# An attention and feed-forward kernel: P divided by products with a diagonal, weight bits decoded by way of PSUM, and two scalars loaded second

## The chip, the cores and the metric

The kernel runs on one core of a Trainium2 chip. The metric is the device time of one execution in microseconds (us). Each program was timed several times; one more execution was recorded by the hardware profiler, and every row shown below is from that record.

## What is computed

The reference in short (sizes of this case: B=4, H=8, S=768, D=64; 3072 tokens, d_model 512, d_ff 2048; n_local 96, n_global 8):

```python
scores = q @ k.T / sqrt(D)
keep = (pos_k < n_global) | ((rel >= 0) & (rel < n_local))      # rel = pos_q - pos_k
scores += -slope[h] * where(is_global & ~is_local, n_local, abs(rel))
a = softmax(where(keep, scores, -1e9))
x = (a @ v) as tokens x (H*D)                                    # 3072 x 512
h = x @ w_in
P = a0 + a1*h + a2*h**2 + a3*h**3
Q = 1 + |b0|*|h| + |b1|*h**2
out = (P / (Q + 1e-6)) @ w_out
```

The two weight matrices arrive as 64-bit floats; the kernel turns their bits into 32-bit floats itself. That is what "decode" means below.

## The kernel before

The work is cut into 96 attention units (u) and 96 feed-forward steps (f). A unit is one block of 128 queries of a pair of heads, in one batch. The blocks i = 0 to 5 of a batch follow each other, and only the block itself and the one before it hold keys to keep, beside the first eight keys. A chunk c is 256 tokens (two blocks, eight units); its feed-forward part is eight steps, each for 256 of the 2048 inner columns. A planner orders the instructions of every engine from priorities: the loop `windowed` runs over t, gives each stage of step t a priority 1000 t plus an offset (`PRI_A` while f is below 8, `PRI` after), and the planner takes what is ready, the lowest number first. The engines then run their lists in order. Step t holds the load of unit t+4, the score and softmax of unit t-2, the transposes of P of unit t-3, the product with V of the pair that ends at t-5, and feed-forward step f = t-12. So attention runs twelve steps ahead, and chunk 0's feed-forward steps fall into t = 12 to 19.

A unit goes like this. `st_load` brings q, k and v by DMA from the SP queue. `st_split` writes each number of q and k as two fp32r numbers (VectorE, then GpSimd at L370). `st_qkT` transposes them on TensorE, `st_qkE` copies them out on ScalarE. `st_score` makes the products (L408), and VectorE adds the mask and takes the row's minimum (L419). `st_soft` is the exponential on ScalarE (L429) and the reciprocal of the row's sum on VectorE (L432, L434). `st_norm` multiplies P by that reciprocal on GpSimd (L441), `st_pT` transposes P on TensorE (L462) and copies it out (L465, ScalarE while u is below 21), `st_pv` multiplies with V (L480). From unit 30 on (RAW) P is copied by a DMA, and its transposes are fp32r.

A feed-forward step: ffn1 (L250 for chunk 0 in fp32, L258 after that in three fp32r products) writes h into a PSUM tile of tag h, of which there are two; `st_ew1` to `st_ew4` make P/Q on ScalarE, VectorE and GpSimd, reading h until L290; ffn2 (L329, later L334) multiplies with w_out.

The weights come as 32 pieces of 128x512. `WSCHED` says in which step t a piece is loaded and decoded: numbers 0 to 5 in t = 0 and 2, 6 to 11 in t = 10, 12 to 17 in t = 11, and 18 to 31 in t = 12 to 18. `MODE` gives for each piece how it is decoded:

- mode 0 and 1: one step on ScalarE (L171), a guard on VectorE (mode 0) or GpSimd (mode 1) (L173), and three steps on VectorE (L174, L176, L178);
- mode 2 and 3: one step on ScalarE (L185), one on GpSimd (mode 2, L187) or ScalarE (mode 3, L189) that writes `low` over the loaded data, and two steps on VectorE (L190, L192).

A loaded piece stands in one of three buffers until its decode has read it. `split_w` later writes each piece as two fp32r pieces (L209, L210) for the chunks from 1 on; these run in step f, by the list `SPLITS`.

`windowed` begins with the loads of units 0 and 2, then n_local and n_global, the identity, the coefficients, two splits and the masks, before the loop. After the loop stands a check of n_local and n_global in small steps on one partition (L679 to L684), which decides whether a general path is run; the planner puts them where VectorE is free.

Of the kernel before, what the change touches and what calls it, by code (L numbers as in the profile page):

```python
# [18 lines left out]
G = 8  # L19
# [4 lines left out]
GBUFS = 3  # L24
RAW = 30
# [11 lines left out]
MODE = (3, 0, 2, 0, 2, 1, 2, 0, 0, 0, 0, 0, 0, 2, 2, 1, 0, 0, 0, 0, 0, 0, 0, 0, 2, 2, 1, 0, 3, 2, 1, 2)  # L37
# [33 lines left out]
def window_masks(nc, scr, mask0, masks, nl, ng):  # L71

    rel, msk, key, g1 = scr
    for n, base in ((0, P), (1, 0)):
# [5 lines left out]
        if n:  # L80
            nc.gpsimd.affine_select(out=rel, in_=rel, pattern=[[-1, P]], base=0, channel_multiplier=1,
                                    compare_op=ALU.is_ge, fill=-BIG)
        nc.vector.tensor_tensor(out=m, in0=rel, in1=msk, op=ALU.add)

    nc.gpsimd.iota(key[:, 0:G], pattern=[[1, G]], base=0, channel_multiplier=0,
                   allow_small_or_imprecise_dtypes=True)
    nc.vector.tensor_scalar(out=g1[:, 0:G], in0=key[:, 0:G], scalar1=ng, scalar2=nl, op0=ALU.is_lt, op1=ALU.mult)
    nc.vector.tensor_scalar(out=g1[:, G:2 * G], in0=key[:, 0:G], scalar1=ng, scalar2=-BIG, op0=ALU.is_ge, op1=ALU.mult)
    nc.vector.tensor_tensor(out=masks[:, 0, 0:G], in0=g1[:, G:2 * G], in1=g1[:, 0:G], op=ALU.subtract)
    nc.vector.tensor_copy(out=mask0, in_=masks[:, 1, :])  # L90
    nc.vector.tensor_tensor(out=mask0[:, 0:G], in0=mask0[:, 0:G], in1=masks[:, 0, 0:G], op=ALU.max)
# [4 lines left out]
def tile_kernel(ctx: ExitStack, tc: tile.TileContext, q, k, v, n_global, n_local,  # L96
# [30 lines left out]
    def st_load(u):  # L127
# [6 lines left out]
        vt = pl.ldp.tile([P, 4, D], F32, tag="vt", name=f"vt{u}", bufs=6)  # L134
        nc.sync.dma_start(out=vt, in_=v[b, hs, r, :].rearrange("h s d -> s h d"))
        nat[u // 2] = n
        vts[u // 2] = vt
# [20 lines left out]
    def decode(src, key):  # L158
# [26 lines left out]
        nc.scalar.activation(out=dst, in_=raw[:, :, 1], func=AF.Abs, scale=2.0 ** -112)  # L185
        if mode == 2:
            nc.gpsimd.tensor_scalar(out=low, in0=half, scalar1=2.0 ** -13, scalar2=FLOOR, op0=ALU.mult, op1=ALU.add)  # L187
        else:
            nc.scalar.activation(out=low, in_=half, func=AF.Copy, scale=2.0 ** -13, bias=FLOOR)  # L189
# [246 lines left out]
    def st_norm(u):  # L436
        i = unit(u)[4]
        pr, st = prob[u]
        for x in range(2):
# [15 lines left out]
    def st_pT(u):  # L455
# [4 lines left out]
        for x in range(2):  # L460
            for w in range(W):
                nc.tensor.transpose(out=t_ps[:, x, w, :], in_=pr[:, x, w, :], identity=ident_r if u >= RAW else ident)  # L462
# [43 lines left out]
    def windowed():  # L506
        st_load(0)
        st_load(2)
        nc.sync.dma_start(out=ni[:, 0:2], in_=n_local.bitcast(I32).partition_broadcast(P))
        nc.sync.dma_start(out=ni[:, 2:4], in_=n_global.bitcast(I32).partition_broadcast(P))  # L510
        make_identity(nc, ident)
        nc.vector.tensor_copy(out=ident_r, in_=ident)
        nc.vector.tensor_copy(out=nf, in_=ni)
        load_coef()
        st_split(0)
        st_split(1)

        nl, ng = nf[:, 0:1], nf[:, 2:3]
        scr = tmp("scr").rearrange("p a (b w) -> p (a b) w", w=P)
        scr = [scr[:, x, :] for x in range(4)]  # L520
        window_masks(nc, scr, mask0, masks, nl, ng)

        base = tc.cur_priority
        for t in range(NU + LAG + F2):
# [8 lines left out]
            if t % 2 == 0:  # L533
                on("load", st_load, t + 4)
            on("score", st_score, t - 2)
# [140 lines left out]
    fl = const.tile([1, 8], F32, name="fl")  # L676
    fi = const.tile([1, 1], I32, name="fi")
    for n, (x, lo, hi) in enumerate(((0, 1.0, 121.0), (1, 0.0, 0.0), (2, 0.0, float(G)), (3, 0.0, 0.0))):
        nc.vector.tensor_scalar(out=fl[:, 4:5], in0=nf[0:1, x:x + 1], scalar1=lo, scalar2=None, op0=ALU.is_ge)  # L679
        nc.vector.tensor_scalar(out=fl[:, 5:6], in0=nf[0:1, x:x + 1], scalar1=hi, scalar2=None, op0=ALU.is_le)  # L680
        nc.vector.tensor_tensor(out=fl[:, n:n + 1], in0=fl[:, 4:5], in1=fl[:, 5:6], op=ALU.mult)
    nc.vector.tensor_tensor(out=fl[:, 4:6], in0=fl[:, 0:2], in1=fl[:, 2:4], op=ALU.mult)
    nc.vector.tensor_tensor(out=fl[:, 6:7], in0=fl[:, 4:5], in1=fl[:, 5:6], op=ALU.mult)
    nc.vector.tensor_copy(out=fi, in_=fl[:, 6:7])  # L684
# [40 lines left out]
```

## Time and profile before

| | |
|---|---|
| time, median of 3 runs | 794.26 us (793.93 to 798.46) |
| time of the profiled execution | 792.2 us |
| its span | 790.4 us |
| TensorE busy | 743.9 us (94%) |
| TensorE weight loads busy | 649.6 us (82%) |
| VectorE busy | 599.6 us (76%) |
| ScalarE busy | 575.1 us (73%) |
| GpSimd busy | 533.3 us (67%) |

The span is the time between the first and the last instruction; the profiled execution's own time holds 1.8 us more. In the rows PE is TensorE, PEld its weight loads, DVE VectorE, ACT ScalarE, POOL GpSimd, SPq the queue that issues the DMAs. A number such as L441 is a line of the kernel. Names of tiles stand without their numbers, so `w_0f` to `w_15f` are decoded pieces, `r` a loaded one, `pr` P, `tp` its transposes. Busy time overlaps: matmuls are pipelined, so what one costs is better read from the distance between starts.

### The profile page before, as it was taken

What the parts mean: (1) busy time and instruction counts of PE and PEld (TensorE: products, weight loads), DVE (VectorE), ACT (ScalarE), POOL (GpSimd) and SP (SyncE); (2) the same over time, 40 slices, a digit from 0 to 9 for tenths busy, and PEclk for the clock granted to TensorE, in tenths of its full rate; (3) what the DMA queues carried; (4) which work ended last, traced back from release to release, by engine and by line L of the source; (5) the groups of instructions that cost most, each with busy time, mean ns of one, the idle gap of its engine ahead of it and who ended that gap; (6) DMA issues with size and microseconds to landing.
All of it is one profiled execution on the core that took longest, in us unless ns stands there. A gap on an engine that the chain in (4) does not pass through costs nothing.

```text
span 790.4 us, 15799 instructions
## 1 busy us (share of the span) xinstructions
PE 743.9 (94%) x5184; PEld 649.6 (82%) x5184; DVE 599.6 (76%) x1453; ACT 575.1 (73%) x1407; POOL 533.3 (67%) x572
## 2 busy tenths in 40 slices
PE   3688978899999999999999999999999999999995
PEld 2467647688998899999899999989999999988993
DVE  5889999987778676777776786777677786776664
ACT  4778677667887777777777777777877777766763
POOL 3868558979877667666667667666677777664440
PEclk9999999899999999999999999999999999999999
DMA  7785445212222233333332332333332332210000
GB/s 183 212 240 173 114 125 189 49 48 54 55 81 68 85 92 87 97 88 86 82 87 82 106 84 81 106 84 82 88 85 77 101 92 78 82 55 14 28 1 32
DMA packets 111932, 72.19 MB, mean 91 GB/s; under 512 B 82912, under 2 KB 97248, under 8 KB 111840
## 3 DMA queue, kind: packets, MB, share of 16 engines
q1 hardware_dynamic: 111840, 71.08, 32.0%
q8 instruction: 44, 0.72, 0.4%
q14 instruction: 48, 0.39, 0.2%
HBM read 35.92 MB, written 6.29 MB: 53 GB/s over the span
## 4 chain that ended last, share of the span: by engine, by line
PE 81%; DVE 6%; POOL 5%; DMA 4%; issue 2%; ACT 1%; SPq 0%; DVEq 0%; POOLq 0%; ACTq 0%
PE h L258 32%; PE acc L334 31%; PE o L480 5%; PE s L408 5%; PE tp L462 3%; PE tk L378 3%; DMA r<-in_moe_w_in_dram 2%; POOL pr L441 2%; PE h L250 1%; POOL sp L370 1%; DMA nat<-in_k_dram 1%; POOL fa L291 1%; DVE pr L419 1%; DVE fu L305 0%; DMA r<-in_moe_w_out_dram 0%
## 5 line engine op out<-in xcount | busy, mean ns | idle before, releaser
L334 PE MATMUL acc<-wout_h,g 128*128 128x512 f32 x704 | 242.8, 403 | 0.8 <-ACT g L313 0.8
L258 PE MATMUL h<-xh,win_h 128*128 128x256 f32 x704 | 205.4, 292 | 1.8 <-DVE fu L290 1.8
L441 POOL TENSOR_SCALAR pr<-pr,stats 128x256 f32<-128x256 f32 (+1 forms) x192 | 178.5, 940 | 39.2 <-issue 12.7
L258 PE MATMUL h<-xl,win_h 128*128 128x256 f32 x704 | 198.7, 282 | 0.0
L291 POOL TENSOR_TENSOR fa<-fa,fs 128x512 f32<-128x512 f32 x95 | 125.1, 1317 | 100.7 <-ACT fs L284 97.4
L334 PEld LDWEIGHTS acc<-wout_h,g 128*128 128x128 f32 x704 | 126.6, 188 | 21.8 <-ACT g L313 1.2
L258 PEld LDWEIGHTS h<-xh,win_h 128*128 128x128 f32 x704 | 133.3, 189 | 10.9 <-issue 6.2
L258 PEld LDWEIGHTS h<-xl,win_h 128*128 128x128 f32 x704 | 133.3, 189 | 2.3 <-issue 0.2
L429 ACT ACTIVATE pr<-pr,stats 128x256 f32<-128x256 f32 (+1 forms) x192 | 93.5, 492 | 53.5 <-DVE stats L419 53.4
L370 POOL TENSOR_TENSOR sp<-nat,sp 128x256 fp32r<-128x256 f32 x96 | 75.8, 790 | 73.5 <-DVE stats L432 41.0
L314 POOL TENSOR_TENSOR g<-fu,g 128x512 fp32r<-128x512 f32 x87 | 112.7, 1295 | 7.7 <-DVE fu L290 4.6
L282 ACT ACTIVATE fu<-h,coef 128x512 f32<-128x512 f32 (+1 forms) x97 | 75.4, 778 | 54.1 <-PE h L258 49.6
L303 DVE SCALAR_TENSOR_TENSOR fu<-fu,coef,q 128x512 f32<-128x512 f32 (+1 forms) x97 | 71.6, 738 | 36.2 <-ACT q L299 35.0
L298 ACT ACTIVATE fs<-fa,coef 128x512 f32<-128x512 f32 (+1 forms) x97 | 70.2, 724 | 30.3 <-POOL fa L291 27.9
L289 DVE TENSOR_TENSOR fu<-fu,h 128x512 f32<-128x512 f32 (+1 forms) x97 | 65.6, 677 | 16.9 <-ACT fs L284 14.9
L465 DVE COPY pT<-tp 128x512 f32<-128x512 f32 (+1 forms) x75 | 48.5, 646 | 35.7 <-PE tp L462 35.0
L369 DVE CAST sp<-nat 128x256 fp32r<-128x256 f32 x96 | 38.3, 399 | 46.7 <-PE tk L378 15.1
L290 DVE SCALAR_TENSOR_TENSOR fu<-fu,coef,h 128x512 f32<-128x512 f32 (+1 forms) x97 | 71.7, 739 | 2.5
L419 DVE CUSTOM_DVE_ANT_0 pr<-s,masks 128x256 f32<-128x256 f32 x160 | 61.4, 420 | 15.2 <-PE s L408 13.3
L408 PE MATMUL s<-kT,qT 128*128 128x256 f32 x384 | 70.5, 305 | 1.8 <-DMA qT<-qT 1.7
L304 DVE SCALAR_TENSOR_TENSOR q<-fa,coef,q 128x512 f32<-128x512 f32 (+1 forms) x97 | 72.1, 744 | 0.0
L408 PEld LDWEIGHTS s<-kT,qT 128*128 128x128 f32 x384 | 61.5, 203 | 9.0 <-DMA qT<-qT 1.9
(273 smaller groups left out, 1658.8 us busy)
## 6 DMA issues: line engine op xcount, KB each, us to landing
raw<-pr SPq DMA_DIRECT2D x58, 256.0 KB
qT<-qT SPq DMA_DIRECT2D x192, 64.0 KB
r<-in_moe_w_in_dram SPq DMA_DIRECT2D x16, 512.0 KB
r<-in_moe_w_out_dram SPq DMA_DIRECT2D x16, 512.0 KB
nat<-in_q_dram SPq DMA_DIRECT2D x48, 128.0 KB
nat<-in_k_dram SPq DMA_DIRECT2D x48, 128.0 KB
vt<-in_v_dram SPq DMA_DIRECT2D x48, 128.0 KB
out_dram<-o SPq DMA_DIRECT2D x24, 256.0 KB
```

What stands on the lines that cost most here:

```text
L258: nc.tensor.matmul(out=hps[f][:, y, :], lhsT=w[:, fs], rhs=x[:, ct, :], start=(n == 0), stop=(n == 3 * NCT - 1))
L282: nc.scalar.activation(out=u, in_=h, func=AF.Identity, scale=a3, bias=a2)
L290: nc.vector.scalar_tensor_tensor(out=u, in0=u, scalar=a1, in1=h, op0=ALU.add, op1=ALU.mult)
L291: side(f).tensor_tensor(out=a, in0=a, in1=s, op=ALU.add)
L303: nc.vector.scalar_tensor_tensor(out=u, in0=u, scalar=a0, in1=r, op0=ALU.add, op1=ALU.mult)
L304: nc.vector.scalar_tensor_tensor(out=r, in0=a, scalar=q1, in1=r, op0=ALU.add, op1=ALU.mult)
L314: side(f).tensor_tensor(out=g[:, 1, ys], in0=u, in1=g[:, 0, ys], op=ALU.subtract)
L334: nc.tensor.matmul(out=acc, lhsT=gs[f][:, z, y, ts], rhs=w, start=(ft == 0 and n == 0), stop=(ft == NFT - 1 and n == 2))
L370: nc.gpsimd.tensor_tensor(out=s[:, :, :, 1, :], in0=n, in1=s[:, :, :, 0, :], op=ALU.subtract)
L408: nc.tensor.matmul(out=s_ps[:, x], lhsT=qT[:, z, x, :], rhs=rhs, start=(z == 0), stop=(z == 1))
L429: nc.scalar.activation(out=d, in_=d, func=AF.Exp, scale=-1.0, bias=st[:, x:x + 1], accum_out=st[:, 2 + 2 * x:3 + 2 * x])
L441: nc.gpsimd.tensor_scalar(out=d, in0=d, scalar1=st[:, 6 + x:7 + x], scalar2=None, op0=ALU.mult)
```

## The change

Four things are changed. (1) For units 0 to 19 (`DIAG`) P is no longer multiplied by the reciprocal on GpSimd: ScalarE scales the identity by it, and the transposes of P become products with that diagonal. (2) Thirteen pieces among numbers 0 to 17 get a mode 4: like mode 3, but `low` is a tile of tag h in PSUM. Of these pieces ten were in mode 0 (1, 3, 7 to 12, 16, 17), two in mode 1 (5, 15) and one in mode 3 (0). (3) n_local and n_global are loaded second, behind q and k of unit 0; the loads of v are a stage of their own, and in the beginning they and the coefficients come behind the masks; the two masks are made in the other order. (4) The check after the loop is done in fewer, wider steps.

```diff
--- before.py
+++ after.py
@@ -22,6 +22,7 @@
 FLOOR = -0.5 + 2.0 ** -14
 TMPS = 6
 GBUFS = 3
+DIAG = 20
 RAW = 30
 LAG = 12
 F2 = 2
@@ -34,7 +35,7 @@
 
 SPLITS = {3: 0, 4: 1, 5: 6, 6: 7, 7: 10, 8: 19, 9: 20, 10: 25, 11: 26, 12: 28, 13: 29, 14: 32}
 
-MODE = (3, 0, 2, 0, 2, 1, 2, 0, 0, 0, 0, 0, 0, 2, 2, 1, 0, 0, 0, 0, 0, 0, 0, 0, 2, 2, 1, 0, 3, 2, 1, 2)
+MODE = (4, 4, 2, 4, 2, 4, 2, 4, 4, 4, 4, 4, 4, 2, 2, 4, 4, 4, 0, 0, 0, 0, 0, 0, 2, 2, 1, 0, 3, 2, 1, 2)
 HI_V = (2, 3, 6, 8, 11, 12, 13, 15, 16, 17, 18, 20, 21, 27, 28, 30, 31)
 LO_V = (0, 2, 4, 5, 7, 8, 10, 13, 16, 17, 18, 20, 21, 22, 23, 24, 25)
 
@@ -71,7 +72,8 @@
 def window_masks(nc, scr, mask0, masks, nl, ng):
 
     rel, msk, key, g1 = scr
-    for n, base in ((0, P), (1, 0)):
+    gm = g1[:, G:2 * G]
+    for n, base in ((1, 0), (0, P)):
         m = masks[:, n, :]
         nc.gpsimd.iota(rel, pattern=[[1, P]], base=-base, channel_multiplier=-1,
                        allow_small_or_imprecise_dtypes=True)
@@ -81,14 +83,17 @@
             nc.gpsimd.affine_select(out=rel, in_=rel, pattern=[[-1, P]], base=0, channel_multiplier=1,
                                     compare_op=ALU.is_ge, fill=-BIG)
         nc.vector.tensor_tensor(out=m, in0=rel, in1=msk, op=ALU.add)
-
-    nc.gpsimd.iota(key[:, 0:G], pattern=[[1, G]], base=0, channel_multiplier=0,
-                   allow_small_or_imprecise_dtypes=True)
-    nc.vector.tensor_scalar(out=g1[:, 0:G], in0=key[:, 0:G], scalar1=ng, scalar2=nl, op0=ALU.is_lt, op1=ALU.mult)
-    nc.vector.tensor_scalar(out=g1[:, G:2 * G], in0=key[:, 0:G], scalar1=ng, scalar2=-BIG, op0=ALU.is_ge, op1=ALU.mult)
-    nc.vector.tensor_tensor(out=masks[:, 0, 0:G], in0=g1[:, G:2 * G], in1=g1[:, 0:G], op=ALU.subtract)
-    nc.vector.tensor_copy(out=mask0, in_=masks[:, 1, :])
-    nc.vector.tensor_tensor(out=mask0[:, 0:G], in0=mask0[:, 0:G], in1=masks[:, 0, 0:G], op=ALU.max)
+        if n == 0:
+            nc.vector.tensor_copy(out=masks[:, 0, 0:G], in_=gm)
+            continue
+
+        nc.gpsimd.iota(key[:, 0:G], pattern=[[1, G]], base=0, channel_multiplier=0,
+                       allow_small_or_imprecise_dtypes=True)
+        nc.vector.tensor_scalar(out=g1[:, 0:G], in0=key[:, 0:G], scalar1=ng, scalar2=nl, op0=ALU.is_lt, op1=ALU.mult)
+        nc.vector.tensor_scalar(out=gm, in0=key[:, 0:G], scalar1=ng, scalar2=-BIG, op0=ALU.is_ge, op1=ALU.mult)
+        nc.vector.tensor_tensor(out=gm, in0=gm, in1=g1[:, 0:G], op=ALU.subtract)
+        nc.vector.tensor_copy(out=mask0, in_=m)
+        nc.vector.tensor_tensor(out=mask0[:, 0:G], in0=mask0[:, 0:G], in1=gm, op=ALU.max)
     nc.vector.tensor_copy(out=masks[:, 2, :], in_=masks[:, 0, :])
 
 
@@ -131,10 +136,12 @@
         n = pl.ldp.tile([P, 2, 4, D], F32, tag="nat", name=f"nat{u}")
         nc.sync.dma_start(out=n[:, 0], in_=q[b, hs, r, :].rearrange("h s d -> s h d"))
         nc.sync.dma_start(out=n[:, 1], in_=k[b, hs, r, :].rearrange("h s d -> s h d"))
-        vt = pl.ldp.tile([P, 4, D], F32, tag="vt", name=f"vt{u}", bufs=6)
-        nc.sync.dma_start(out=vt, in_=v[b, hs, r, :].rearrange("h s d -> s h d"))
         nat[u // 2] = n
-        vts[u // 2] = vt
+
+    def st_load_v(u):
+        c, t, p, b, i = unit(u)
+        vt = vts[u // 2] = pl.ldp.tile([P, 4, D], F32, tag="vt", name=f"vt{u}", bufs=6)
+        nc.sync.dma_start(out=vt, in_=v[b, 2 * p:2 * p + 4, i * P:(i + 1) * P, :].rearrange("h s d -> s h d"))
 
 
     win_h = const.tile([P, NCT, DF], FR, name="win_h")
@@ -183,6 +190,9 @@
 
 
         nc.scalar.activation(out=dst, in_=raw[:, :, 1], func=AF.Abs, scale=2.0 ** -112)
+        if mode == 4:
+
+            low = pl.ps_h.tile([P, 2 * TOK], I32, tag="h", name="l" + name)
         if mode == 2:
             nc.gpsimd.tensor_scalar(out=low, in0=half, scalar1=2.0 ** -13, scalar2=FLOOR, op0=ALU.mult, op1=ALU.add)
         else:
@@ -436,6 +446,12 @@
     def st_norm(u):
         i = unit(u)[4]
         pr, st = prob[u]
+        if u < DIAG:
+            dg = pl.att.tile([P, 2, 2, P], F32, tag="raw", name=f"dg{u}", bufs=1)
+            for x in range(2):
+                nc.scalar.activation(out=dg[:, x, 0, :], in_=ident, func=AF.Identity, scale=st[:, 6 + x:7 + x])
+            prob[u] = (pr, dg)
+            return
         for x in range(2):
             d = blocks_of(pr[:, x], i)
             nc.gpsimd.tensor_scalar(
@@ -459,7 +475,10 @@
         t_ps = pl.ps_t.tile([P, 2, 2, P], FR if u >= RAW else F32, tag="t", name=f"tp{u}")
         for x in range(2):
             for w in range(W):
-                nc.tensor.transpose(out=t_ps[:, x, w, :], in_=pr[:, x, w, :], identity=ident_r if u >= RAW else ident)
+                if u < DIAG:
+                    nc.tensor.matmul(out=t_ps[:, x, w, :], lhsT=pr[:, x, w, :], rhs=st[:, x, 0, :], start=True, stop=True)
+                else:
+                    nc.tensor.transpose(out=t_ps[:, x, w, :], in_=pr[:, x, w, :], identity=ident_r if u >= RAW else ident)
         pT = pl.att.tile([P, 2, 2, P], F32, tag="pT", name=f"pT{u}", bufs=2)
         t_ps = t_ps.bitcast(F32) if u >= RAW else t_ps
         (nc.scalar.copy if u < EARLY else nc.vector.tensor_copy)(out=pT[:, :, 0:W, :], in_=t_ps[:, :, 0:W, :])
@@ -505,20 +524,21 @@
 
     def windowed():
         st_load(0)
-        st_load(2)
         nc.sync.dma_start(out=ni[:, 0:2], in_=n_local.bitcast(I32).partition_broadcast(P))
         nc.sync.dma_start(out=ni[:, 2:4], in_=n_global.bitcast(I32).partition_broadcast(P))
+        st_load(2)
         make_identity(nc, ident)
         nc.vector.tensor_copy(out=ident_r, in_=ident)
+        st_split(0)
         nc.vector.tensor_copy(out=nf, in_=ni)
-        load_coef()
-        st_split(0)
-        st_split(1)
-
         nl, ng = nf[:, 0:1], nf[:, 2:3]
         scr = tmp("scr").rearrange("p a (b w) -> p (a b) w", w=P)
         scr = [scr[:, x, :] for x in range(4)]
+        st_split(1)
         window_masks(nc, scr, mask0, masks, nl, ng)
+        st_load_v(0)
+        st_load_v(2)
+        load_coef()
 
         base = tc.cur_priority
         for t in range(NU + LAG + F2):
@@ -532,6 +552,7 @@
 
             if t % 2 == 0:
                 on("load", st_load, t + 4)
+                on("load", st_load_v, t + 4)
             on("score", st_score, t - 2)
             on("soft", st_soft, t - 2)
             on("ffn1a", st_ffn1, f, 0)
@@ -673,15 +694,17 @@
         windowed()
 
 
-    fl = const.tile([1, 8], F32, name="fl")
+    fl = const.tile([1, 4], F32, name="fl")
     fi = const.tile([1, 1], I32, name="fi")
-    for n, (x, lo, hi) in enumerate(((0, 1.0, 121.0), (1, 0.0, 0.0), (2, 0.0, float(G)), (3, 0.0, 0.0))):
-        nc.vector.tensor_scalar(out=fl[:, 4:5], in0=nf[0:1, x:x + 1], scalar1=lo, scalar2=None, op0=ALU.is_ge)
-        nc.vector.tensor_scalar(out=fl[:, 5:6], in0=nf[0:1, x:x + 1], scalar1=hi, scalar2=None, op0=ALU.is_le)
-        nc.vector.tensor_tensor(out=fl[:, n:n + 1], in0=fl[:, 4:5], in1=fl[:, 5:6], op=ALU.mult)
-    nc.vector.tensor_tensor(out=fl[:, 4:6], in0=fl[:, 0:2], in1=fl[:, 2:4], op=ALU.mult)
-    nc.vector.tensor_tensor(out=fl[:, 6:7], in0=fl[:, 4:5], in1=fl[:, 5:6], op=ALU.mult)
-    nc.vector.tensor_copy(out=fi, in_=fl[:, 6:7])
+    lim = const.tile([1, 2, 4], F32, name="lim")
+    nc.gpsimd.memset(lim, 0.0)
+    for x, w, val in ((0, 0, 1.0), (1, 0, 121.0), (1, 2, float(G))):
+        nc.gpsimd.memset(lim[:, x, w:w + 1], val)
+    nc.vector.tensor_tensor(out=fl, in0=nf[0:1], in1=lim[:, 0], op=ALU.is_ge)
+    nc.vector.tensor_tensor(out=lim[:, 0], in0=nf[0:1], in1=lim[:, 1], op=ALU.is_le)
+    nc.vector.tensor_tensor(out=fl, in0=fl, in1=lim[:, 0], op=ALU.mult)
+    nc.vector.tensor_reduce(out=lim[:, 1, 0:1], in_=fl, op=ALU.min, axis=mybir.AxisListType.X)
+    nc.vector.tensor_copy(out=fi, in_=lim[:, 1, 0:1])
     stands = nc.values_load(fi[0:1, 0:1], min_val=0, max_val=1)
     with tc.If(stands < 1):
         with ExitStack() as es:
```

## Rows read from the trace of the kernel before

**Rows 1.** Stretches: us; busy us of PE, PEld, DVE, ACT, POOL; clock, DMA share, GB/s

```profile
10.00:50.00 40.00, 25.04 (x122) 19.48 (x123) 34.42 (x122) 27.01 (x89) 27.42 (x34) 1.00 0.81 227
50.00:80.00 30.00, 26.18 (x150) 21.55 (x149) 28.10 (x68) 23.86 (x59) 22.65 (x24) 0.94 0.67 191
80.00:120.00 40.00, 35.25 (x168) 22.23 (x167) 38.79 (x90) 28.03 (x70) 21.96 (x24) 1.00 0.47 130
120.00:150.00 30.00, 25.40 (x162) 19.28 (x160) 29.10 (x60) 23.08 (x55) 28.32 (x23) 1.00 0.42 127
...
160.00:790.00 630.00, 621.08 (x4546) 558.56 (x4544) 457.32 (x1082) 464.20 (x1114) 422.08 (x452) 1.00 0.26 74
```

**Rows 2.** Chain that ended last, 0 to 160 us: start, us, what

```profile
22.53 1.22 POOL pr L441
...
31.49 1.24 POOL w_2f L173
...
36.53 3.69 POOL pr L441 x3
```

**Rows 3.** Stretches, L441 alone: us, GpSimd busy (instructions)

```profile
0.00:155.00 155.00, 45.73 (x40) 0.97 0.58 162
```

**Rows 4.** Decode steps by line to 155 us (min/median/max ns); ScalarE's timeline

```profile
L173 DVE TENSOR_SCALAR w_0f<-w_0f x3: 400/500/672, 17.1 to 56.3; 128x512 f32<-128x512 f32 x3
...
L174 DVE TENSOR_SCALAR w_0f<-w_0f x3: 421/609/828, 17.8 to 57.6; 128x512 int32<-128x512 int32 x3
...
L190 DVE SCALAR_TENSOR_TENSOR r<-r x11: 678/682/695, 15.3 to 142.0; 128x512 int32<-128x512 int32 x11
...
L189 ACT ACTIVATE r<-r x2: 654/664/673, 14.6 to 127.3; 128x512 int32<-128x512 uint16 x2
...
L303 DVE SCALAR_TENSOR_TENSOR fu<-fu,coef,q x9: 730/735/743, 75.5 to 154.4; 128x512 f32<-128x512 f32 x9
...
13.98 0.68 ACT L185 ACTIVATE w_0f<-r 128x512 f32<-128x512 f32 x1 [0.18 <-DMA r<-in_moe_w_in_dram]
...
73.15 0.70 ACT L171 ACTIVATE w_2f<-r 128x512 f32<-128x512 f32 x1
```

**Rows 5.** Timeline of ScalarE: start, us, instruction (count)

```profile
6.13 0.45 ACT L392 ACTIVATE qT<-tk 128x128 fp32r<-128x128 f32 x2 [4.13 <-PE tk L378]
...
6.46 0.38 ACT L395 CAST kT<-tk 128x256 fp32r<-128x256 f32 x1
...
15.12 0.38 ACT L429 ACTIVATE pr<-pr,stats 128x128 f32<-128x128 f32 x1
```

**Rows 6.** Timeline of TensorE, two places where it runs without a gap

```profile
75.62 3.62 PE L250 MATMUL h<-x,w_1f 128*128 128x256 f32 x16
78.89 0.83 PE L408 MATMUL s<-kT,qT 128*128 128x256 f32 x4
...
169.19 0.60 PE L462 MATMUL tp<-ident,pr 128*128 128x128 f32 x4
169.54 0.51 PE L334 MATMUL acc<-wout_h,g 128*128 128x512 f32 x1
```

**Rows 7.** TensorE's timeline at the lead-in's end; the stretch behind it

```profile
150.88 0.69 PE L462 MATMUL tp<-ident,pr 128*128 128x128 f32 x2 [3.31 <-POOL pr L441]
...
151.00:157.00 6.00, 5.98 (x27) 5.58 (x28) 6.00 (x16) 3.62 (x12) 5.91 (x5) 0.51 0.29 66
```

**Rows 8.** Waits, 0 to 60 us: us in total, times, longest

```profile
POOL sp L370 <- DVE fl L680: 3.1, 1, 3.1
```

**Rows 9.** Timelines: ffn1 on TensorE, and one decode on ScalarE and VectorE

```profile
51.20 3.53 PE L250 MATMUL h<-x,w_0f 128*128 128x256 f32 x8
...
60.41 0.69 ACT L185 ACTIVATE w_4f<-r 128x512 f32<-128x512 f32 x1 [1.92 <-DMA r<-in_moe_w_out_dram]
...
65.67 1.06 DVE L192 SCALAR_TENSOR_TENSOR w_4f<-w_4f,r 128x512 int32<-128x512 int32 x1
...
68.44 5.25 PE L250 MATMUL h<-x,w_1f 128*128 128x256 f32 x16 [2.03 <-DVE fu L290]
```

## The prediction

> **What bounds the kernel now.** I read the busy time by stretch first [rows 1]. From 160 us to the end TensorE is busy 621.1 of 630 us, and nothing in that stretch is edited (the diagonal serves units 0 to 19, the changed decode modes the pieces up to number 17), so those 630 us stay and the case is the lead-in. There no engine is full all the way. From 10 to 50 us TensorE has 25.0 of 40 us, VectorE 34.4, GpSimd 27.4 and the DMA engines are busy 0.81 of the time; from 50 to 150 us VectorE is the wall with 28.1 of 30, 38.8 of 40 and 29.1 of 30 us, and in the last of these GpSimd stands beside it with 28.3 of 30. ScalarE is the one with room: 27.0 of 40, 23.9 of 30, 28.0 of 40, 23.1 of 30.
>
> Then the chain that ended last [rows 2]: before 50 us it goes three times through GpSimd steps that the change removes, two normalisations (1.22 and 3.69 us) and the guard of one decode (1.24 us), 6.15 us in all. The normalisation, L441, is 45.7 us of GpSimd's time in the first 155 us, forty instructions, exactly units 0 to 19 [rows 3].
>
> Last, the end of the lead-in [rows 7]: at 150.88 us a transpose has made TensorE wait 3.31 us for L441, and in the stretch behind it, 151 to 157 us, the granted clock is 0.51 (1.2 GHz of 2.4). Some 6 us at half clock are 3 us of work lost, so this place costs about 6.3 us.
>
> **The change part by part.** *Normalisation.* The forty L441 go (45.7 us of GpSimd). In their place ScalarE scales a 128x128 identity, twice a unit. The trace has no such operation. Nearest below: two copies of 128x128 out of PSUM in 0.45 us, whose successor starts 0.33 us after the first, so 0.17 each; nearest above: an exponential of 128x128 with a bias pointer and a sum, 0.38 us [rows 5]. I take 0.2 (it has no sum to read out): forty make 8 us, bounds 6.6 to 15. The diagonal has one buffer, so the scaling of a unit waits in ScalarE's order for the previous unit's products, and behind it stand exponentials and the copies of pT; the products of a unit come a step earlier in the order than the next scaling, so I put that at 0, and at up to 0.2 us a unit if the cover goes (4 us).
>
> On TensorE 72 transposes become real fp32 products. Four transposes go by in 0.35 us (169.19 to 169.54), 0.0875 each, one instruction each; an fp32 product of 256 columns is two instructions, sixteen instructions (eight products) in 3.27 us (75.62 to 78.89), 0.41 a product, so about 0.204 for 128 columns [rows 6]. The addition is 72 x 0.117 = 8.4 us of TensorE, double at half clock. The stages have TensorE room of 15, 4, 5 and 5 us [rows 1], so I take +1.5 us on the path, bounds 0 and +8.4. The Trainium skill, "TensorE: Matmul & The Clock Gate", section Terms, speaks against the change: transpose mode is "4× faster for FP32". By it the addition would be the 18.9 us of the rival below; the rows say 2.3 times, and the sum goes by them.
>
> *Decode.* Thirteen pieces go to the new mode; their first ScalarE steps stand between 13.98 and 73.15 us now [rows 4]. Ten of them were in mode 0 and lose two VectorE steps, the guard (L173, 0.40 clean, median 0.50 over w_0f) and the shift (L174, 0.42 and 0.61): 0.82 to 1.11 us each. Two were in mode 1 and lose the shift there and the guard on GpSimd. That is 9 to 12.3 us of VectorE. The two steps that stay now read `low` in PSUM: L303, with a PSUM operand, takes 0.735 us where L190 takes 0.682 [rows 4], so 26 x 0.053 = 1.4 us come back; net 7.6 to 10.9, I take 8.5. ScalarE gets one more step a piece, at L189's 0.664 us [rows 4]: twelve (one had it) make 8 us. Below nothing is not possible for VectorE here, since no step is added to it.
>
> The price that no row shows is the buffer. `low` takes one of the two PSUM buffers of tag h, which hold ffn1's output from 51.20 us on [rows 9]. TensorE already waits 2.03 us for one at 68.44 us. A decode now in a like place holds its piece from 60.41 us to the end of its last VectorE step at 66.73 us, 6.3 us (same rows). Pieces 12 and 15 to 17 come late enough to meet ffn1. I take +1 us, since their VectorE steps get a shorter queue; bounds 0 and +8 (four waits of 2 us).
>
> *Loads and small steps.* n_local and n_global pass four issues on the SP queue (v of unit 0, and q, k and v of unit 2); coef and v go behind the masks. The masks are ready that much sooner, and the end check has five small VectorE steps in place of fifteen; GpSimd now waits 3.1 us for one of them (L680) before a split [rows 8]. The weight loads run into 81% busy DMA engines right behind, so I take 0.5 us, bounds 0 and 1.5. Unit 2's q and k are two issues later and one earlier (v of unit 0), under the same cover; without it, that one issue. The four memsets at the end check stand on GpSimd, which loses 45.7 us; nothing.
>
> **The sum by stage.** 10 to 50 us: GpSimd leaves the chain (6.15 us) but ScalarE takes more. The pieces are spread over 14 to 73 us, so about eight fall here (one of them has its step already), and of the forty scalings, spread over 155 us, about ten: 7 x 0.66 + 10 x 0.2 = 6.7 us. It stands at 33.7 of 40, beside DMA at 0.81. I take -3.5 with the small steps, bounds 0 and -6. 50 to 80 us: VectorE loses some 4 us, ScalarE, with five pieces and eight scalings, goes to 23.9 + 3.3 + 1.6 = 28.8 of 30 and becomes the late one: -1, bounds 0 and -3. 80 to 150 us: by the same share some 20 us of GpSimd go, and ScalarE gets only 3.6; VectorE keeps all its steps, but steps waiting behind decodes (splits, later pieces) can run in the room it has won before 80 us, and steps stretched while GpSimd is at work (L174 0.42 to 0.83) shrink: -5, bounds -1 and -9. End of the lead-in: no L441 to wait for, and no half clock if something else isn't late in the same place; VectorE is, partly: -4, bounds 0 and -6.3. With +1.5 for TensorE and +1 for the buffers: -11 us.
>
> The profiled execution took 792.2 us, so 781.2; the median of the runs shown is 2.06 us above it, so I predict 783 us.
>
> **The rivals.** *ScalarE takes VectorE's place* (23%). It gains 16 us of work, 11.6 of them before 80 us, where it was at 51 of 70. For it: it would be at 33.7 of 40 and 28.8 of 30, and it takes its steps in order, weight loads among what they wait for. Against: after 80 us it has room. Then nothing is won before 80 us and half of it behind, with the same two costs: -2.5 - 2 + 2.5 = -2, 792 us.
>
> *The whole lead-in closes up* (13%). All bounds on the good side but TensorE's and the buffers' terms: -6 - 3 - 9 - 6.3 + 1.5 = -23, 771 us. For it: three engines lose work at once. Against: DMA is busy 0.81 early, and 40 us can't become less than 32.
>
> *The products are as dear as four transposes* (6%). At 0.35 us, the time that the row has for four of them, TensorE gets 72 x 0.26 = 18.9 us; with room of 29 us spread unevenly I put 6 of them on the path in place of 1.5: -6.5, 788 us. For it: a product loads its weights twice; against it: 0.204 us by the sixteen instructions.
>
> *The buffers of tag h decide* (12%). A decode that holds a buffer while its VectorE steps queue leaves ffn1 one buffer, and a ScalarE step that waits for one holds the exponentials behind it. Four such pieces in series at 6.3 us, less the 2.03 that ffn1 waits already, are 4 x 4.3 = 17 us, in place of the 1 in the sum; and the gain ahead of 50 us (3.5) goes with it, since ScalarE's queue carries the exponentials: -11 - 1 + 17 + 3.5 = +8.5, 803 us. It decides from the point at which the late pieces land after ffn1's first products, as they do now (51 against 54 to 73 us); against it, a decode freed of two steps lands sooner.
>
> That the diagonal or the PSUM tile would not be used isn't open: both stand in the code. What is open is that the planner orders the engines anew, which the ranges carry.
>
> **How the numbers follow.** The forecast has 46% and its own range 776 to 790. About 1% (7.9 us) is what a measurement of this kernel can tell from no change: the three runs lie 0.6% apart. Below 786.3 us lie nine tenths of the forecast (0.41), the closed lead-in (0.13) and a little of the dear products (0.02): 0.56. Above 802.2 us lie most of the buffer case and a tail: 0.10. The rest, 0.34, is within. The range is 772 to 798: it takes in the forecast, the ScalarE and product cases and about half of the closed lead-in, and leaves out some 2 in 10.
>
> **What would show it.** L441 starts with unit 20, so its count falls by forty. The products of units 0 to 19 appear as two instructions each, 0.2 us a product. Two ScalarE steps a unit of 128x128 at about 0.2 us. From 10 to 80 us ScalarE is above 0.9 and VectorE below it; behind 80 us VectorE leads. ffn1 starts some 3 us before 51 us. TensorE is full from about 145 us on, without the half clock at 151 to 157 us. Waits of ScalarE's `low` step for a release of h, or of ffn1 for L192, above 2 us each would show the buffer rival. Wrong would be: a lead-in of 155 us still, or a steady part that is not 630 us.

## The result, and the profile after

The changed kernel takes 797.41 us (median of 12 runs, 796.02 to 799.19) and the kernel before 794.1 on the same chip: a ratio of 1.0044, interval 1.0028 to 1.0060. I predicted 783.0 and most of the chance for faster. The time lies inside the range and on the other side of no change. The profiled execution has a span of 796.6 us, against 790.4 before: the two that were profiled lie 6.2 us apart, the medians 3.3, so the rows below show the loss somewhat large.

The stretches after (us; busy us of PE, PEld, DVE, ACT, POOL with instructions; granted clock, DMA share, GB/s) answer to [rows 1]:

```profile
10.00:50.00 40.00, 22.30 (x107) 18.55 (x107) 25.71 (x81) 32.56 (x104) 9.20 (x14) 0.86 0.88 248
50.00:80.00 30.00, 23.45 (x164) 19.82 (x163) 26.09 (x71) 26.83 (x73) 9.44 (x13) 0.85 0.81 234
80.00:120.00 40.00, 34.71 (x157) 24.91 (x156) 37.67 (x75) 29.73 (x72) 16.41 (x18) 0.91 0.44 125
120.00:150.00 30.00, 28.46 (x147) 19.15 (x146) 27.79 (x62) 20.87 (x55) 19.56 (x19) 1.00 0.20 47
150.00:160.00 10.00, 10.00 (x76) 8.45 (x75) 7.92 (x19) 6.43 (x19) 5.58 (x6) 1.00 0.20 44
160.00:790.00 630.00, 628.16 (x4606) 565.38 (x4604) 451.80 (x1091) 471.11 (x1136) 417.13 (x451) 1.00 0.27 74
```

Read the last row first. From 160 us on TensorE is full, as it was, but 4606 matmuls stand there and not 4546: the lead-in has left more behind. The stretch at half clock at 151 us [rows 7] is gone, so the end of the lead-in looks as predicted. The loss is at its start: from 10 to 50 us TensorE is busy for 22.3 us in place of 25.0 and from 50 to 80 us for 23.5 in place of 26.2, at a lower granted clock in both, though from 10 to 50 us VectorE went from 34.4 to 25.7 and GpSimd from 27.4 to 9.2. ScalarE went up, to 32.6 of 40, and the DMA engines from 0.81 to 0.88.

TensorE's and ScalarE's timelines after show what it looks like (start, us, instruction; in brackets the idle time before it and what ended it):

```profile
18.31 0.98 PE L418 MATMUL s<-kT,qT 128*128 128x256 f32 x3 [3.43 <-DMA qT<-qT]
...
33.42 0.66 ACT L192 ACTIVATE w_1f<-r 128x512 f32<-128x512 f32 x1 [1.23 <-DMA r<-in_moe_w_in_dram]
...
36.05 0.68 ACT L192 ACTIVATE w_1f<-r 128x512 f32<-128x512 f32 x1
36.62 0.69 ACT L452 ACTIVATE dg<-ident,stats 128x128 f32<-128x128 f32 x2
37.21 0.62 ACT L199 ACTIVATE lr<-r 128x512 int32<-128x512 uint16 x1
...
37.07 0.80 PE L479 MATMUL tp<-dg,pr 128*128 128x128 f32 x2 [4.51 <-ACT dg L452]
...
63.26 1.13 PE L260 MATMUL h<-x,w_0f 128*128 128x256 f32 x4
66.50 1.13 PE L260 MATMUL h<-x,w_0f 128*128 128x256 f32 x4 [2.12 <-DVE w_2f L202]
...
74.09 1.05 PE L479 MATMUL tp<-dg,pr 128*128 128x128 f32 x8
74.90 0.72 PE L418 MATMUL s<-kT,qT 128*128 128x256 f32 x4
```

TensorE no longer waits for GpSimd's normalisation; it waits 4.51 us for ScalarE's diagonal, ahead of which stand, beside exponentials, copies and a split, two decode steps, one of which first waited for its weights. ffn1 starts at 63.26 us, not at 51.20 [rows 9], but the experiments will show that this start doesn't go with the time. L441, now L457, is down to 152:

```profile
L457 POOL TENSOR_SCALAR pr<-pr,stats 128x256 f32<-128x256 f32 (+1 forms) x152 | 131.3, 874 | 35.2 <-issue 11.3
```

### The profile page after: what moved, and what is told of

It is laid out like the page before. It is cut to its first block, busy times and chain, and to the rows that moved or that the text cites. A ratio compares the mean times of both kernels' runs of the same rounds, so it can differ in the third digit from the quotient of the medians.

```text
span 796.6 us, 15899 instructions
## 1 busy us (share of the span) xinstructions
PE 748.9 (94%) x5256; PEld 657.6 (83%) x5256; DVE 582.2 (73%) x1422; ACT 590.5 (74%) x1459; POOL 480.7 (60%) x534
## 4 chain that ended last, share of the span: by engine, by line
PE 86%; DVE 6%; DMA 4%; issue 2%; ACT 1%; SPq 1%; POOL 0%; POOLq 0%; DVEq 0%; ACTq 0%
PE h L268 33%; PE acc L344 31%; PE s L418 5%; PE o L499 5%; PE tk L388 3%; PE tp L481 3%; PE acc L339 2%; PE h L260 2%; DMA r<-in_moe_w_in_dram 2%; PE tp L479 1%; DMA qT<-qT 1%; DVE pr L429 1%; DMA r<-in_moe_w_out_dram 0%; DMA ni<-in_n_global_dram 0%; DVE q L314 0%
## 5 line engine op out<-in xcount | busy, mean ns | idle before, releaser
L457 POOL TENSOR_SCALAR pr<-pr,stats 128x256 f32<-128x256 f32 (+1 forms) x152 | 131.3, 874 | 35.2 <-issue 11.3
L380 POOL TENSOR_TENSOR sp<-nat,sp 128x256 fp32r<-128x256 f32 x96 | 74.0, 771 | 99.4 <-DVE sp L379 44.4
L379 DVE CAST sp<-nat 128x256 fp32r<-128x256 f32 x96 | 32.5, 339 | 51.2 <-PE tk L388 16.8
```

The source lines that it names most:

```text
L380: nc.gpsimd.tensor_tensor(out=s[:, :, :, 1, :], in0=n, in1=s[:, :, :, 0, :], op=ALU.subtract)
L457: nc.gpsimd.tensor_scalar(out=d, in0=d, scalar1=st[:, 6 + x:7 + x], scalar2=None, op0=ALU.mult)
```

## The experiments

Ratios are to the kernel before on the same chip. The change has three parts, and each was first run by itself. In the expectations a letter names a theory; what it says stands beside it.

**The parts alone.** The diagonal alone, the decode alone, the new opening alone (loads, masks and end check):

```diff
 order_only: after with    DIAG = 0 and the MODE of before
 diag_only:  before with   the diagonal (DIAG = 20, st_norm, st_pT)
 mode_only:  before with   the new MODE and mode 4
```

> The changed kernel without the diagonal and with the old decode modes: only the order of the loads and the end check are new. Three theories of the loss. A (products): the second passes of 72 real products on TensorE, about 8 us, are the loss; then this run is at the kernel before or up to 3 us faster. B (ScalarE's queue): the scalings and the low steps stand in line behind weight loads; the same. C (loads): qT's transfer of unit 1 now waits behind two weight loads (6.0 us on the chain); then this run alone is 3 to 6 us slower than before.

Measured 799.18 us, 1.0063 (1.0043 to 1.0084).

> The kernel before with the diagonal alone. Theory A (products): 8.4 us more TensorE work less what leaves GpSimd, so 3 to 8 us slower than before. Theory B (ScalarE's queue): slower by 2 to 6 us, with waits of the products for the scaling of 2 to 5 us each before 60 us. Theory C (loads): faster by some 3 to 8 us, as the sum of the prediction had it for the normalisation.

Measured 788.5 us, 0.9925 (0.9897 to 0.9953). ffn1 starts at 46.30 us.

> The kernel before with the thirteen mode 4 pieces alone. Theory A (products): faster by 2 to 6 us, VectorE's saving. Theory B (ScalarE's queue): between 2 us faster and 2 us slower. A fourth theory, D (buffers of tag h): ffn1 starts after 55 us and TensorE waits above 2 us for the last step of a decode; 3 to 8 us slower than before.

Measured 790.54 us, 0.9946 (0.9925 to 0.9967).

Two parts win, 6 and 4 us, and the opening, for which I had taken half a microsecond of gain, loses 5. A plain sum of the three is -0.7 - 0.5 + 0.6%, so 789 us; the whole change measures 797. Some 1.1% are lost between the parts.

**The products.** The changed kernel with the diagonal set to 0 or 1 by a comparison in place of the reciprocal, and P through plain transposes. P stays undivided in units 0 to 19; the scalings on ScalarE remain.

```diff
-nc.tensor.matmul(out=t_ps[:, x, w, :], lhsT=pr[:, x, w, :], rhs=st[:, x, 0, :], start=True, stop=True)
+nc.tensor.transpose(out=t_ps[:, x, w, :], in_=pr[:, x, w, :], identity=...)
```

> The changed kernel, but for units 0 to 19 the reciprocal is replaced by a comparison that gives 1.0, so the diagonal is the identity, and P goes through it as a transpose: P stays undivided in these units. Every step and wait of ScalarE and VectorE stays; only the second pass of 72 products is gone. Theory A (products): 5 to 9 us faster than the changed kernel, so 789 to 792 us. Theories B, C and D: within 2 us of the changed kernel's 797.4 us.

Measured 796.03 us, 1.0024 (1.0003 to 1.0045). That is 1.4 us below the changed kernel, and the two intervals overlap. This kernel is also planned anew, which by the last runs below is worth some 4 us, so the price of the second passes isn't measured. But the 5 to 9 us of theory A aren't there, and the diagonal alone, with the same 72 products, is faster than before: they don't carry the loss.

**The opening, taken apart.** Before with the new loads alone, with the new end check alone, with the new order of the masks alone:

```diff
 windowed(), loads_only:
 st_load(0)
-st_load(2)
 nc.sync.dma_start(out=ni[:, 0:2], ...)
 nc.sync.dma_start(out=ni[:, 2:4], ...)
+st_load(2)
...
 window_masks(nc, scr, mask0, masks, nl, ng)
+st_load_v(0)
+st_load_v(2)
+load_coef()
```

> The kernel before with the new opening alone: n_local and n_global second, the splits and the coefficients in their new places, v as a load of its own behind the masks; old masks, old end check. Theory E: unit 1's split now stands behind the cast of n_local and the mask steps on VectorE, and unit 1's scores come 2 us later; the whole loss of the order sits here, 3 to 6 us slower than before. Theory F: the planner's order of the lead-in is so sensitive that any small edit moves the time by some us either way; then this run may lie anywhere from -5 to +6 us, and the three parts don't add up to the +4.5 us of the order alone.

Measured 798.66 us, 1.0062 (1.0042 to 1.0082): the whole loss of the opening.

> The kernel before with the new end check alone (five small VectorE steps and four memsets on GpSimd in place of fifteen steps). Theory E: at the kernel before or up to 2 us faster. Theory F: a shift of 2 us or more in either direction.

Measured 793.98 us, 0.9998 (0.9977 to 1.0019).

> The kernel before with the new order of the masks alone (mask of the block itself first, the global columns behind it). Theory E: within 1.5 us of the kernel before. Theory F: a shift of 2 us or more in either direction.

Measured 794.27 us, 1.0005 (0.9982 to 1.0028).

Something else tells these three apart. Set instruction by instruction against before, ScalarE's list stands in the same order in the check's and the masks' kernel (2492 of 2492), and so does SP's (1004 and 1005 of 1005). With the new loads every engine has the instructions of before, but the planner orders the lead-in anew: 2303 of 2492 and 954 of 1005 can be lined up in the same order. (About half of either list is the general path, which isn't run and doesn't change.)

The trace with the new loads, TensorE's timeline at the start:

```profile
8.61 0.75 PE L380 MATMUL tk<-ident_r,sp 128*128 128x128 f32 x4 [2.77 <-POOL sp L372]
...
18.40 0.98 PE L410 MATMUL s<-kT,qT 128*128 128x256 f32 x3 [3.76 <-DMA qT<-qT]
```

And before:

```profile
7.35 0.75 PE L378 MATMUL tk<-ident_r,sp 128*128 128x128 f32 x4 [1.26 <-POOL sp L370]
...
16.40 0.98 PE L408 MATMUL s<-kT,qT 128*128 128x256 f32 x3 [1.74 <-DMA qT<-qT]
```

So 2 us are lost in the first 20, and unit 1's split stands behind mask steps on VectorE. Whether these 2 us are a part of the 5 was not separated.

**The pair.** The diagonal and the decode together, with the opening of before:

> The kernel before with the diagonal and the new decode modes, without the new order of loads, masks and end check. Alone the two gave 788.5 and 790.5 us beside 794.7. If the loss is the new order (theory C), this run is the change without it: 780 to 786 us if the two gains add, 786 to 790 if both take the same slack (ScalarE's). If the two disturb each other (ScalarE's queue, theory B, or the buffers of tag h, theory D), it is at 794 us or above.

Measured 794.61 us, 1.0008 (0.9989 to 1.0027). The gains of 6 and 4 us are gone, and of the 0.44% that the whole change loses, 0.36% come with the opening on top of the pair. ScalarE is at 35.78 of 40 us from 10 to 50 us, and ffn1 starts at 65.11 us. Two theories stood: ScalarE's line is closed (B), or the PSUM buffers of tag h are (D). Four kernels tell them apart: the same with `low` in SBUF; with the thirteen `low` on GpSimd; with the diagonal made on GpSimd; and the SBUF form of the decode without the diagonal.

```diff
-MODE = (4, 4, 2, 4, 2, 4, 2, 4, ...)
+MODE = (3, 3, 2, 3, 2, 3, 2, 3, ...)      dm_mode3, mode3_only (the latter without the diagonal)
+MODE = (2, 2, 2, 2, 2, 2, 2, 2, ...)      dm_mode2
-nc.scalar.activation(out=dg[:, x, 0, :], in_=ident, func=AF.Identity, scale=st[:, 6 + x:7 + x])
+nc.gpsimd.tensor_scalar(out=dg[:, x, 0, :], in0=ident, scalar1=st[:, 6 + x:7 + x], ...)      dm_dgpool
```

> The kernel before with the diagonal and the new decode, but the decode's low words stay in the loaded buffer in SBUF and not in a PSUM buffer of tag h; ScalarE has the same steps. Theory D (the h buffers eat the two gains): the gains of the diagonal alone (788.5) and of the decode alone (790.5) add up, 783 to 787 us, and no wait of over 1 us stands between a decode step and an ffn1 product. Theory B (ScalarE's queue eats them): 793 to 796 us as with both (794.6), ScalarE again above 35 of 40 us from 10 to 50 us.

Measured 793.79 us, 1.0003 (0.9985 to 1.0021). D falls: without the h buffers the gains don't come back, though ffn1 starts at 54.60 us.

> The kernel before with the diagonal, and the thirteen pieces decoded with their low words made by GpSimd in SBUF: ScalarE loses 13 steps of 0.66 us, GpSimd, which the diagonal has freed of 46 us, gets them; no h buffer is used. Theory B: ScalarE falls to some 28 to 31 of 40 us from 10 to 50 us and the gains add up, 782 to 787 us. Theory D says the same of the time, so this run is read together with the one that leaves the steps on ScalarE: if that one stays at 794 and this one falls, it is ScalarE. A third theory, G (neither: VectorE slows down beside GpSimd, or the loads set the pace): 790 us or more here too.

Measured 794.6 us, 1.0008 (0.9988 to 1.0027).

> The kernel before with the diagonal and the new decode by way of PSUM, but the diagonal is made on GpSimd, not on ScalarE: ScalarE loses forty steps of some 0.3 us (12 us). Theory B: 785 to 790 us, and products wait for the diagonal less than the 11.5 us in 60 that they wait now. Theory D: 793 to 796 us, as with both.

Measured 792.94 us, 0.9997 (0.9979 to 1.0015). B falls too, as a matter of ScalarE's work: 7 or 9 us less of it from 10 to 80 us, in either way, gives nothing that can be measured. (Each of these kernels is also planned anew, which by the last runs below is worth some 4 us. The theories stood to win 7 to 13 us, with the diagonal on GpSimd 5 to 10; one kernel alone could hide the smaller of these, three hardly.)

> The kernel before with the thirteen pieces decoded like the new mode, the low words in the loaded buffer in SBUF: no diagonal, no h buffer. Against the new decode alone (790.5 us, ffn1's first product at 61.45 us behind a VectorE decode step): theory D puts the late ffn1 down to the h buffers, so 785 to 788 us and ffn1's first product before 56 us; theory B has nothing to gain from the buffers here, 789 to 792 us and ffn1's first product still near 61 us.

Measured 791.45 us, 0.9977 (0.9959 to 0.9995). ffn1 starts at 49.37 us, where it starts at 61.45 in the decode alone. So ffn1 starts later where the h buffers are used, by 12 us here and by 10.5 with the diagonal, but the time doesn't follow: the kernel with the late start gains 4 us, this one 2.

What became of the microseconds that ScalarE was given back is in its timeline. The stretch 10 to 80 us, the pair and then the pair with `low` on GpSimd:

```profile
10.00:80.00 70.00, 50.34 (x277) 44.06 (x278) 55.66 (x175) 60.84 (x179) 19.95 (x30) 0.76 0.83 241
```

```profile
10.00:80.00 70.00, 47.98 (x255) 41.69 (x255) 58.55 (x170) 52.29 (x157) 31.24 (x41) 0.93 0.81 233
```

ScalarE's work falls from 60.84 to 52.29 us, by 8.55. In a stretch of fixed length its idle time grows by as much; what the traces add is where. Its waits for weight loads in these 70 us, added up over its timeline, rise from 3.45 us (4 waits) to 12.10 (9 waits), by 8.65. With the diagonal on GpSimd it works 6.8 us less (54.05) and waits 4.6 us more (8.03). In the kernel with `low` on GpSimd the longest are these:

```profile
52.67 0.66 ACT L186 ACTIVATE w_1f<-r 128x512 f32<-128x512 f32 x1 [2.45 <-DMA r<-in_moe_w_out_dram]
54.97 0.66 ACT L186 ACTIVATE w_4f<-r 128x512 f32<-128x512 f32 x1 [1.64 <-DMA r<-in_moe_w_out_dram]
...
67.87 0.67 ACT L172 ACTIVATE w_7f<-r 128x512 f32<-128x512 f32 x1 [1.79 <-DMA r<-in_moe_w_out_dram]
70.29 0.67 ACT L172 ACTIVATE w_8f<-r 128x512 f32<-128x512 f32 x1 [1.75 <-DMA r<-in_moe_w_out_dram]
```

A decode step stands at the head of ScalarE's line before its weights are there, and copies, exponentials and diagonals of the attention wait behind it. That these waits are why nothing is won isn't shown: the pair itself has only 3.45 us of them, less than the 7.0 us of before, and wins nothing either. Why the weights aren't there was not tested; that the loads set the pace (theory G of an expectation) stays possible, with the DMA engines busy 0.92 of the time from 10 to 50 us in the pair and 0.87 with `low` on GpSimd, against 0.81 before.

**Holding the weights back.** A faster decode frees the load buffers sooner. On SP's queue the 20th weight load stands behind the q transposes of 13 units before, of 11 with the pair (the 10 of the expectation is the 19th). So the next theory was that the weights crowd out the attention. A one-column copy into the load buffer ties the loads of pieces 6 to 23 to finished units (with the copies that mark these, 34 small steps more on GpSimd):

```diff
+if held is not None:
+    nc.gpsimd.tensor_copy(out=raw[:, 0, 0:1], in_=mark[:, held:held + 1])
 nc.sync.dma_start(out=raw.bitcast(I32), in_=src...)
```

> The kernel before with the diagonal and the new decode, and pieces 6 to 23 held back: a one-column GpSimd copy of a finished unit's sum is written into the load buffer ahead of the load, so that the load of a piece can't be issued before that unit's softmax. On SP's queue the 20th weight load stands then behind 14 units' q transposes in place of 10 (before: 13), the last behind 19 in place of 17 (before: 20.5). Theory L (the faster decode frees the load buffers sooner, so the planner queues weights ahead of attention, which is the slow chain of the lead-in): 785 to 789 us, the two gains add up or nearly. Rival G (the sheer work and the chain's latencies cancel the gains, the queue's order is a by-product): 793 us or more.

Measured 795.09 us, 1.0001 (0.9989 to 1.0013).

> The same hold on the kernel with the diagonal and the thirteen low words on GpSimd (794.6 without the hold, its last weight load behind 16 units): theory L 784 to 789 us, with ScalarE below 32 of 40 us from 10 to 50 us; rival G 793 us or more. Against the held kernel with the decode by way of PSUM it shows what ScalarE's thirteen steps are worth once the order is back: 0 to 3 us.

Measured 796.17 us, 1.0023 (1.0008 to 1.0038).

> The same hold on the whole change (797.4 without it): the 20th weight load stands behind 13.5 units in place of 11, the last behind 18 in place of 17. Theory L: 789 to 793 us, so that what is left against the held kernel without the new opening is the opening's own loss of some 3 to 5 us. Rival G: 796 us or more.

Measured 803.58 us, 1.0111 (1.0094 to 1.0127).

> The same hold on the kernel with the new opening alone, without the diagonal and the new decode (799.2; there the weights also crept ahead, the last load behind 18 units in place of 20.5; held, behind 22). Theory L: the opening's loss is the weights' order too, so 792 to 796 us. Rival O (the opening loses by what it does in the first 20 us, unit 1's split and its q transposes coming 2 us late): 798 to 802 us.

Measured 804.32 us, 1.0116 (1.0097 to 1.0134).

The theory isn't borne out: nothing of the 6 to 10 us comes back. It isn't out altogether, since the hold's own price on the kernel before wasn't run, and it brings a new order too. With the hold the pair's attention is ahead (the 14th unit's transposes at 66.7 us, 73.9 without), but ffn1 is later, 73 us against 65, and the time is the same. With the new opening the hold makes the kernels 0.5 to 0.7% slower, some 4 to 6 us.

**The order alone.** Last, one number of the planner, which adds and removes no instruction (one copy of an output tile moves from ScalarE to VectorE), in the kernel before and in the one with the diagonal alone:

```diff
-ew4=850, ew2=2400, ffn2a=-400, pT=850, ffn2b=2050, dec=1850, wsplit=1090)
+ew4=850, ew2=2400, ffn2a=-400, pT=850, ffn2b=2050, dec=1950, wsplit=1090)
```

> The kernel before with one number of the planner changed: the decode's place in a step goes from 1850 to 1950, behind the first chain step of the next but one stage. No instruction is added or removed; TensorE's list differs in 1042 of some 10,200 lines, ScalarE's in 567. Theory N (any new order of the lead-in costs or gives some 4 us by itself, and the order of before is a tuned one): 797 to 801 us. Rival M (the work carries the time, a new order of the same work costs nothing that shows): 793 to 796 us, ratio within 0.2% of 1.

Measured 798.0 us, 1.0051 (1.0028 to 1.0073); nine of the twelve runs lie at 796.9 to 799.4 us, three at 794.5 to 795.0.

> The same changed number in the kernel before with the diagonal alone (788.5 in its own order). Theory N: the gain of 6 us was partly an order that came out well, so 792 us or more, and the gain over the replanned kernel before differs from 6 us. Rival M: 787 to 790 us, the gain of 0.75% stands in this order too.

Measured 792.99 us, 0.9993 (0.9972 to 1.0013).

The same work in another order costs 4 us: nearly as much as the opening, and about as much as the smaller gain. ScalarE's and TensorE's timelines of the replanned kernel before show one place:

```profile
53.05 0.66 ACT L171 ACTIVATE w_3f<-r 128x512 f32<-128x512 f32 x1 [2.90 <-DMA r<-in_moe_w_out_dram]
53.62 0.60 ACT L209 CAST wout_h<-w_2f 128x512 fp32r<-128x512 f32 x1
56.41 0.67 ACT L171 ACTIVATE w_0f<-r 128x512 f32<-128x512 f32 x1 [2.19 <-DMA r<-in_moe_w_out_dram]
57.68 0.67 ACT L185 ACTIVATE w_1f<-r 128x512 f32<-128x512 f32 x1 [0.60 <-DMA r<-in_moe_w_out_dram]
58.25 0.43 ACT L392 ACTIVATE qT<-tk 128x128 fp32r<-128x128 f32 x2
58.56 0.38 ACT L395 CAST kT<-tk 128x256 fp32r<-128x256 f32 x1
...
59.04 1.09 PE L462 MATMUL tp<-ident,pr 128*128 128x128 f32 x4 [6.10 <-ACT kT L395]
```

TensorE stands for 6.10 us behind a copy of kT that needs 0.38 us. What it copies was made by products that start at 52.24 us, but three decode steps stand ahead of it that wait for weights. From 10 to 80 us ScalarE waits 18.3 us for weights here and 7.0 us before. In the other kernels of new order and old work it is the same: 15.8 us with the new loads alone, and with the diagonal 10.2 us replanned against 2.8. In the two that kept the order it stays at 7.4 (check) and 7.5 (masks).

This mark isn't in every slow kernel. Over the same 70 us the whole change has 6.1 us of it and the pair 3.5, less than before, and the slowest of all, the hold on the new opening (804.32 us), has 5.5. So it goes with the loss of the replanned kernel and of the new loads. How the whole change loses it doesn't show.

And the diagonal gains under both settings of that number: under the new one 0.9993 / 1.0051 = 0.994, 4.6 us, under the old one 6. That speaks for a gain of the work, though two orders are few, and each kernel has its own.

## Why the prediction was wrong

**The bound.** Right: the stretch from 160 us is untouched, and the lead-in decides.

**The operations.** Right in kind, and mostly in size. Forty L441 went. Eight instructions of four products take 0.81 us (74.09 to 74.90), so 0.203 each (0.23 in the kernel with the diagonal alone, eight in 0.91); I took 0.204. The Trainium skill, "TensorE: Matmul & The Clock Gate", section Terms, has transpose mode four times faster for FP32; measured against the 0.0875 us of a transpose [rows 6] the products take 2.3 to 2.6 times as long, and the sum was right to go by the rows. Their extra passes were to cost 1.5 us on the path; that they cost 1.4 isn't shown, since that difference is within the noise and within what a new order is worth. The scaling takes 0.30 us and not 0.2 (two from 36.62 to 37.21), inside its bounds. The half clock at 151 us went, and with it the wait for L441. But from 151 to 157 us the clock is 1.00 also in the decode alone and in the opening alone, which keep L441, and of these one is faster than before and one slower, so the worth of that place, put at 4 us, isn't shown. ScalarE gained 15.4 us over the span, where I had 16. VectorE's saving was mis-sized: 13.9 us by the decode alone (599.6 to 585.7 us), forecast 7.6 to 10.9. The 1.4 us for `low` in PSUM did not come, as the last section shows.

**The gain of each edit.** The sum of -11 comes near what the diagonal and the decode win by themselves, 6 and 4 us. Given what an order alone is worth, that is in part luck.

**The first step that failed: "Loads and small steps", -0.5 us, bounds 0 and 1.5 of gain.** I weighed what the moved instructions wait for and left out any loss. The check and the masks are worth nothing that can be measured, the loads cost 5 us. These come with a new order of the whole lead-in, and a new order alone has about the same price (1.0051 against 1.0062) and the same mark in the trace, decode steps that wait for weights at the head of ScalarE's line. That the opening has no price besides, such as the late q transposes at 18.40 us, isn't shown.

**The second: the sum by stage.** I added gains of two edits as if the queues around them stood still, and gave the planner's new order to "the ranges". From 10 to 50 us the sum had -3.5 and from 50 to 80 us -1; the changed kernel's TensorE was instead busy 2.7 us less in each. The two gains cancel: in five ways of doing the pair (794.6, 793.8, 794.6, 792.9, 795.1 us) the time is that of before, and in a sixth, held with `low` on GpSimd (796.2), it is 0.2% above. "ScalarE takes VectorE's place" was the rival nearest to it with 792 us, but for a reason that half fell: it isn't the amount of ScalarE's work, since 8.55 us less of that won nothing. That it is its line, which takes its steps in a set order, isn't shown for the pair. My "ScalarE above 0.9 from 10 to 80" is 0.85 in the changed kernel. That 797.4 lies inside 772 to 798 is luck: no case of the prediction has a cost of the loads, and the only one with a time above it, 803 us, is that of the buffers.

**The h buffers.** The rival is out as to the time: taking them away gives 0.05% by the ratios, inside the interval. Its sign is there, a later ffn1, but costs nothing that shows.

**Still open.** Adding the decode to the diagonal costs 0.8%, and merely replanning the diagonal costs 0.7%, so the pair's loss has the size of a new order. That it is one, and not something that the two edits do to each other, isn't shown: an order that gives the pair its 10 us was not found. Nor was any kernel here faster than the diagonal alone, 788.5 us, in the order of before.

## What to carry to other kernels

Where a planner makes the order of in-order queues, time a change of its order alone before pricing small edits. Here that is 0.5%, so each part has to be run by itself, its gain or loss is even then known only to within what an order is worth, and gains don't add. Look whether the order stayed; the two edits that kept it changed nothing (0.9998 and 1.0005).

## What the hardware showed that I had not expected

Work taken off ScalarE won nothing. That its idle time grew is arithmetic; unexpected was that the growth stood in front of weight loads, 8.65 us of it against 8.55 us less work, 4.6 against 6.8 in the other kernel. And a low granted clock early on didn't decide: the decode alone has 0.72 from 50 to 80 us and wins 4 us, the replanned kernel before has 0.89 there and loses 4.

A VectorE step that reads one operand from PSUM was no slower here, and steadier. In the decode alone the last decode step, which reads `low` in PSUM (`lr`), takes 0.676 to 0.687 us in all thirteen pieces. In the SBUF form of the same decode (mode3_only), where it reads `low` in the loaded buffer (`r`), the same instruction on the same shape takes up to 1.2 us in these two groups:

```profile
L195 DVE SCALAR_TENSOR_TENSOR w_0f<-w_0f,lr x4: 676/679/687, 16.0 to 51.4; 128x512 int32<-128x512 int32 x4
L195 DVE SCALAR_TENSOR_TENSOR w_1f<-w_1f,lr x3: 679/680/682, 35.4 to 42.4; 128x512 int32<-128x512 int32 x3
...
L192 DVE SCALAR_TENSOR_TENSOR w_0f<-w_0f,r x5: 677/693/1226, 16.7 to 53.2; 128x512 int32<-128x512 int32 x5
L192 DVE SCALAR_TENSOR_TENSOR w_1f<-w_1f,r x5: 692/849/1208, 35.1 to 55.7; 128x512 int32<-128x512 int32 x5
```

(Count; then shortest, median and longest in ns, and the first and last start.) What stretches some of the others was not tested.
